# Merging float64 weights on VectorE with one instruction in place of three, with ScalarE and GpSimd preparing sign and low bits

## The chip, the cores and the metric

The kernel runs on one core of one Trainium2 chip. The metric is device time in microseconds (us); lower is better. One program does the whole computation. Its engines are PE (TensorE), DVE (VectorE), ACT (ScalarE), POOL (GpSimd) and SP (SyncE, which here issues every DMA). Each engine executes its own instructions strictly in the order in which the program holds them, and waits at an instruction until the semaphores it names have arrived, so whatever stands behind a waiting instruction on the same engine waits too.

## The reference

Attention with a threshold under the row maximum, for 8 batches of 8 heads with 576 positions of 64 values, and then a two-layer network with softplus in the middle on the 4608 resulting rows:

```python
scores = scale * np.matmul(q, k.transpose(0, 1, 3, 2))
thresh = np.max(scores, axis=-1, keepdims=True) - tau
scores = np.where(scores >= thresh, scores, -1000000000.0)
attn = np.exp(scores - max) / (sum + 1e-09)
attn_out = np.matmul(attn, v).astype(np.float32)
x = attn_out.transpose(0, 2, 1, 3).reshape(4608, 512)
h = x @ w_in                                  # w_in  512 x 2048, float64
g = np.maximum(h, 0.0) + np.log1p(np.exp(-np.abs(h)))
out = (g @ w_out).astype(np.float32)          # w_out 2048 x 512, float64
```

The two weight matrices come as float64, because they were divided by the square root of a numpy number. q, k and v are float32. The engines have no float64, so the kernel has to make float32 values out of the two 32-bit words of each weight.

## The kernel before, in words

**Attention.** The work is cut into 32 units of one batch and two heads. A unit has 9 tiles of 128 query rows, so there are 288 tiles, numbered through. A tile goes through these steps: scores on PE into one of two PSUM buffers called s (`scores`, L410); the negated row maximum `negm` on DVE (`row_max`, L416) and the threshold `thr`; the exponential into `e_all` on ACT (`exps`, L424); the mask and the row sum on DVE (`mask`, L429, which writes `e_all` again); the transpose of the masked weights on PE (`weights_T`, L460 and L463); copies of the transposed weights into a rounded part gH on ACT and a remainder gL (`weights_hi`, `weights_lo`); and the products with v on PE (`values`, L536 to L538). In the first 36 tiles (`TG = 36`) `thr` and the copies of gL are ACT's (L418, L483) and the remainder itself is made on PE (L511, L513: tile `tl`). From tile 36 on, gL and `thr` are DVE's (L125, L420), ACT copies gH alone (L485), and the transposes go back into the s buffer, which is free for the scores of a later tile only when gH and gL have been read out of it.

**The network.** From tile 41 on the matrix products of the two layers (L629 to L633 with `w_in`, L687 to L691 with `w_out`) are laid between the attention steps, a quota of them for every tile. Softplus is on ACT (L651) and needs another activation table than the exponential, hence the table loads around it.

**The weights.** The matrices are prepared in 32 blocks of 128x512 values, 16 of `w_in` (tiles `wc_i`, `wa_i`) and 16 of `w_out` (`wc_o`, `wa_o` or `ws_o`, `wo_o`). A new block is begun at every second tile, tiles 0 to 62, by the step "w" of a written order of steps per tile. `to_f32` loads the raw words of the block into `wc` by one DMA (L177) and then works in steps that are put off by a number of points (`defer`; there are two points in each of the first 36 tiles). Each weight has a high word (sign, exponent, upper bits of the fraction) and a low word. Before the change a block took:

- ACT, L185: the absolute value of the high word, read as a float32 and scaled, into `wa`;
- POOL, L186: a clamp of `wa` between two limits;
- DVE, L192: shift `wa` left by 3, which puts exponent and fraction in their float32 places;
- DVE, L194: take the sign bit out of the high word and put it in by a bitwise or;
- DVE, L197: shift the low word right by 29, so that three bits remain, and put them in by a bitwise or;
- POOL, L118 and L125: split the float32 value into the rounded part and the remainder that PE multiplies with. For `w_in` both are stored to a buffer in memory (SP, L226), from which the network loads them later (L613).

**What sets the order.** The code writes the steps of a tile in a fixed sequence, but a scheduler then lays out the instructions of each engine by its own estimates of when each could run. A changed instruction therefore moves its neighbours too, on all engines. The merging instructions on DVE are tied behind the last mask that was written (`behind(i, masked)`), which keeps them from being laid ahead of it.

## Time and profile before

| what | value |
|---|---|
| median of 3 runs | 1471.95 us (1471.4 to 1474.29) |
| the profiled execution's own time | 1474.09 us |
| its span, from the first to the last instruction | 1472.3 us |
| mean granted TensorE clock | 0.991 |
| busy share of the span: PE, DVE, ACT, POOL | 95%, 69%, 59%, 41% |
| HBM read and written | 140.51 MB, 27.41 MB |

In the groups of the profile a row reads: line, engine, operation, output tile, inputs, shapes, count, then busy time in us and the mean of one in ns, then the idle time of the engine just before and what ended it. Rows of windows give for each stretch of the span its length, the busy time of each engine with the number of instructions, the granted clock of PE (1.00 is full), the share of time in which the DMA engines were busy, and GB/s. Rows of waits read: engine, line, what it waited for, us in total, number of times, the longest. Rows of the timeline begin with the start and the duration in us. PE's matmuls are pipelined, so that the durations of neighbours overlap.

### The profile page before, as it was taken

The page shows a single profiled execution, that of the slowest core. Times are in us where ns is not written, and L with a number is a line of the kernel's source. Part 1 is how long each engine was busy: PE and PEld are TensorE (multiplying, and loading weights), DVE is VectorE, ACT ScalarE, POOL GpSimd, SP SyncE. Part 2 cuts the span into 40 slices and gives each one's busy share as a digit, 9 for nine tenths or more (in the row PEclk, how much of TensorE's full clock was granted, in tenths as well). Part 3 has the DMA queues.
Part 4 walks back from the last instruction along what each step waited for, and adds up shares of the span by engine and source line. Part 5 has one row for each costly group of instructions (what it writes and reads, how often), then busy time and mean ns, then how long its engine had stood idle before and what let it go on. Part 6 is the DMA issues. An engine that isn't in the chain of part 4 may idle for free.

```text
span 1472.3 us, 23929 instructions
## 1 busy us (share of the span) xinstructions
PE 1405.8 (95%) x8024; PEld 1192.3 (81%) x8024; DVE 1013.3 (69%) x2251; ACT 872.2 (59%) x1671; POOL 604.7 (41%) x629
## 2 busy tenths in 40 slices
PE   6878789999999999999999999999999999999998
PEld 5767677788888888888888888888888888788886
DVE  6998778877777777777777777777777777411211
ACT  6887577566766576656666666657665665411110
POOL 3767565544333433343334433343334332323221
PEclk9999899999999999999999999999999999999999
DMA  5777565434344554335334534454433533344321
GB/s 149 213 203 199 168 200 161 134 111 135 109 121 117 129 150 121 110 107 153 108 101 116 140 106 117 117 139 142 119 113 107 159 93 82 101 136 128 116 86 43
DMA packets 131210, 189.95 MB, mean 129 GB/s; under 512 B 35312, under 2 KB 86800, under 8 KB 131088
## 3 DMA queue, kind: packets, MB, share of 16 engines
q1 hardware_dynamic: 131088, 188.43, 44.2%
q8 instruction: 64, 1.05, 0.3%
q14 instruction: 58, 0.48, 0.1%
HBM read 140.51 MB, written 27.41 MB: 114 GB/s over the span
## 4 chain that ended last, share of the span: by engine, by line
PE 74%; DVE 8%; ACT 7%; issue 4%; POOL 3%; DMA 3%; SPq 1%; POOLq 0%; DVEq 0%; ACTq 0%
PE s L410 10%; PE h L631 8%; PE h L629 8%; PE h L633 8%; PE o L691 7%; PE o L689 7%; PE o L687 7%; PE s L463 7%; PE pv L536 3%; PE pv L537 3%; DVE negm L416 2%; PE tr L351 2%; DVE e_all L429 2%; POOL g L125 1%; DMA wc_i<-in_moe_w_in_dram 1%
## 5 line engine op out<-in xcount | busy, mean ns | idle before, releaser
L485 ACT CAST gH<-s 128x512 fp32r<-128x512 f32 (+1 forms) x448 | 186.7, 466 | 160.8 <-PE s L463 152.8
L125 POOL TENSOR_TENSOR g<-st,g 128x512 fp32r<-128x512 f32 x144 | 192.8, 1357 | 194.2 <-DVE g L122 182.3
L429 DVE SCALAR_TENSOR_TENSOR e_all<-s,thr,e_all 128x576 f32<-128x576 f32 x288 | 234.3, 815 | 37.8 <-ACT e_all L424 34.8
L416 DVE TENSOR_REDUCE negm<-s 128x1 f32<-128x576 f32 x288 | 217.4, 755 | 41.4 <-PE s L410 33.4
L691 PE MATMUL o<-wo_o,g 128*128 128x512 f32 x576 | 232.6, 404 | 5.3 <-POOL g L125 5.3
L631 PE MATMUL h<-xl,wi 128*128 128x512 f32 x576 | 233.1, 405 | 1.7 <-POOL xl L125 1.7
L687 PE MATMUL o<-wo_o,g 128*128 128x512 f32 x576 | 232.9, 404 | 1.0 <-ACT st L651 0.7
L629 PE MATMUL h<-xh,wi 128*128 128x512 f32 x576 | 230.6, 401 | 1.9 <-ACT st L651 1.4
L633 PE MATMUL h<-xh,wi 128*128 128x512 f32 x576 | 230.4, 400 | 0.0
L689 PE MATMUL o<-wo_o,g 128*128 128x512 f32 x576 | 229.7, 399 | 0.0
L424 ACT ACTIVATE e_all<-s,negm 128x576 f32<-128x576 f32 x288 | 215.8, 750 | 10.3 <-DVE negm L416 6.5
L125 DVE TENSOR_TENSOR gL<-s,gH 128x512 fp32r<-128x512 f32 (+1 forms) x280 | 175.0, 633 | 59.1 <-ACT gH L485 55.8
L410 PE MATMUL s<-kT,qT 128*128 128x288 f32 x1024 | 194.3, 311 | 13.3 <-DVE gH L125 5.9
L410 PEld LDWEIGHTS s<-kT,qT 128*128 128x128 f32 x1024 | 150.5, 192 | 33.9 <-issue 11.4
L122 DVE CAST g<-st 128x512 fp32r<-128x512 f32 x128 | 57.4, 485 | 149.6 <-ACT st L651 149.1
L463 PE MATMUL s<-identr,e_all 128*128 128x128 f32 x1008 | 155.7, 277 | 3.8 <-DVE e_all L429 3.8
L651 ACT ACTIVATE st<-h 128x512 f32<-128x512 f32 x144 | 78.3, 596 | 117.3 <-PE h L633 116.7
L536 PE MATMUL pv<-gH,vt 128*128 128x320 f32 (+1 forms) x512 | 143.9, 301 | 1.4 <-ACT gH L485 1.3
L537 PE MATMUL pv<-gL,vt 128*128 128x320 f32 (+1 forms) x512 | 142.8, 300 | 1.5 <-DVE gL L125 1.4
L691 PEld LDWEIGHTS o<-wo_o,g 128*128 128x128 f32 x576 | 108.7, 189 | 29.6 <-POOL g L125 11.0
L463 PEld LDWEIGHTS s<-identr,e_all 128*128 128x128 f32 x1008 | 116.2, 142 | 19.2 <-DVE e_all L429 10.9
L629 PEld LDWEIGHTS h<-xh,wi 128*128 128x128 f32 x576 | 108.9, 189 | 25.4 <-ACT st L651 1.9
(105 smaller groups left out, 2381.1 us busy)
## 6 DMA issues: line engine op xcount, KB each, us to landing
wi<-wi_d SPq DMA_DIRECT2D x144, 512.0 KB
qT<-qT SPq DMA_DIRECT2D x124, 128.0 KB
R<-r_d SPq DMA_DIRECT2D x64, 144.0 KB
kn<-in_k_dram SPq DMA_DIRECT2D x32, 256.0 KB
qn<-in_q_dram SPq DMA_DIRECT2D x32, 256.0 KB
vn<-in_v_dram SPq DMA_DIRECT2D x32, 256.0 KB
wc_i<-in_moe_w_in_dram SPq DMA_DIRECT2D x16, 512.0 KB
wi_d<-wc_i SPq DMA_DIRECT2D x32, 256.0 KB
```

The costliest lines, as they stand in the source:

```text
L125: eng.tensor_tensor(out=out_, in0=in_, in1=hi.bitcast(F32), op=ALU.subtract)
L410: nc.tensor.matmul(sp[:, hf, 0:HS], lhs, s.kT[j][:, k0 + hf * HS:k0 + (hf + 1) * HS], start=(m == 0), stop=(m == len(parts) - 1))
L416: nc.vector.reduce_max(negm, s.sp[t][:, :, 0:HS], axis=AX.XY, negate=True)
L424: nc.scalar.activation(e_all[:, s.half[t], :].rearrange("p (h n) -> p h n", h=2), s.sp[t][:, :, 0:HS], AF.Exp, bias=s.m[t][0], scale=1.0)
L429: masked.append(nc.vector.scalar_tensor_tensor(out=e2, in0=s.sp[t][:, :, 0:HS], scalar=s.m.pop(t)[1], in1=e2, op0=ALU.is_ge, op1=ALU.mult, ...
L463: nc.tensor.matmul(main[:, c, :], e[:, c0:c0 + P], ident, is_transpose=True, start=True, stop=True)
L629: nc.tensor.matmul(h, wi[:, 0, cc, :], u.h[cc], start=(cc == 0), stop=False)
L631: nc.tensor.matmul(h, wi[:, 0, cc, :], u.l[cc], start=False, stop=False)
L633: nc.tensor.matmul(h, wi[:, 1, cc, :], u.h[cc], start=False, stop=(cc == NCC - 1))
L687: nc.tensor.matmul(o, gh[:, sl], wo[fc][:, 0, :], start=(i == 0), stop=False)
L689: nc.tensor.matmul(o, gh[:, sl], wo[fc][:, 1, :], start=False, stop=False)
L691: nc.tensor.matmul(o, gl[:, sl], wo[fc][:, 0, :], start=False, stop=(i == QF - 1))
```

## The change

The low word of each weight is turned in place into a word that holds the sign in bit 31 and the three bits in bits 0 to 2. It is done by halves of 16 bits: ACT computes the low half from the high half (a scaled and rounded value, which is the three top bits), and POOL then writes the high half from a comparison of the high word with zero (32768 or 0). DVE shifts `wa` by 3 and merges the prepared word in the same instruction. The sequence per block is now: ACT L191 (low half), one point later ACT L195 (absolute value, as L185 before), POOL L196 (high half) and POOL L198 (clamp, as L186 before), `step` points later DVE L203 (the one merge), one point later the split on POOL. Before, the three DVE instructions were one point, `step` points and `step` points apart; `step` is 2 for the first blocks and 1 once half of the `w_out` pieces are held.

```diff
+    third = cpool.tile([P, 1], F32, name="third")
+    nc.vector.memset(third, 2.0 ** -14 - 0.5)
...
+        halves = words.bitcast(U16).rearrange("p (n t) -> p n t", t=4)
         words = words.rearrange("p (n t) -> p n t", t=2)
-        low, high = words[:, :, 0], words[:, :, 1]
+        low, high = words[:, :, 0], words[:, :, 1].bitcast(F32)
         mu = m.bitcast(U32)
         def first():
-            nc.scalar.activation(m, high.bitcast(F32), AF.Abs, scale=2.0 ** 16)
+            nc.scalar.activation(halves[:, :, 0], halves[:, :, 1], AF.Identity, scale=2.0 ** -13, bias=third)
+            later_(1, magnitude)
+
+        def magnitude():
+            nc.scalar.activation(m, high, AF.Abs, scale=2.0 ** 16)
+            nc.gpsimd.tensor_scalar(out=halves[:, :, 1], in0=high, scalar1=0.0, scalar2=32768.0,
+                                    op0=ALU.is_lt, op1=ALU.mult)
             nc.gpsimd.tensor_scalar(out=m, in0=m, scalar1=W_MAX, scalar2=W_MIN, op0=ALU.min, op1=ALU.max)
-            later_(1, lambda: second(0))
-        def second(n):
-            if n == 0:
-                i = nc.vector.tensor_scalar(out=mu, in0=mu, scalar1=3, scalar2=None, op0=ALU.logical_shift_left)
-            elif n == 1:
-                i = nc.vector.scalar_tensor_tensor(out=mu, in0=high, scalar=0x80000000, in1=mu,
-                                                   op0=ALU.bitwise_and, op1=ALU.bitwise_or)
-            else:
-                i = nc.vector.scalar_tensor_tensor(out=mu, in0=low, scalar=29, in1=mu,
-                                                   op0=ALU.logical_shift_right, op1=ALU.bitwise_or)
+            later_(step, second)
+
+        def second():
+            i = nc.vector.scalar_tensor_tensor(out=mu, in0=mu, scalar=3, in1=low,
+                                               op0=ALU.logical_shift_left, op1=ALU.bitwise_or)
             if took > 1:
                 behind(i, masked)
-            if n < 2:
-                later_(step, lambda: second(n + 1))
-            else:
-                later_(1, lambda: then(parts, w, done))
+            later_(1, lambda: then(parts, w, done))
```

Behind the changed lines all line numbers are larger by 3 in the changed kernel (the mask is L432 there, the exponential L427, gH L486, the split L122 and L129).

DVE's order around tile 4 of unit 4 (tile 40 of all), where gL and gH on DVE empty an s buffer that PE's next scores wait for. Before:

```order
L550 TENSOR_TENSOR xp_4_2042<-pv_4_0_2043,xp_4_2042 64x256
L429 SCALAR_TENSOR_TENSOR e_all_136,sums_4_1865<-s_1_138,thr_4_3_2034,e_all_136 128x576
L197 SCALAR_TENSOR_TENSOR wa_o5_1946<-wc_o5_1945,wa_o5_1946 128x512
L192 TENSOR_SCALAR wa_o6_2016<-wa_o6_2016 128x512
L416 TENSOR_REDUCE negm_4_4_2073<-s_0_137 128x1
L125 TENSOR_TENSOR gL_4_1_2031<-s_1_138,gH_4_1_2030 128x4x128
L420 TENSOR_SCALAR thr_4_4_2074<-negm_4_4_2073,ntau_85 128x1
L125 TENSOR_TENSOR gH_4_1_2030<-s_1_138,gH_4_1_2030 64x128 x2
L429 SCALAR_TENSOR_TENSOR e_all_136,sums_4_1865<-s_0_137,thr_4_4_2074,e_all_136 128x576
L194 SCALAR_TENSOR_TENSOR wa_o6_2016<-wc_o6_2015,wa_o6_2016 128x512
```

And the same place in the changed kernel:

```order
L432 SCALAR_TENSOR_TENSOR e_all_138,sums_4_1870<-s_1_140,thr_4_3_2037,e_all_138 128x576
L553 TENSOR_TENSOR xp_4_2046<-pv_4_0_2047,xp_4_2046 64x256
L419 TENSOR_REDUCE negm_4_4_2078<-s_0_139 128x1
L423 TENSOR_SCALAR thr_4_4_2079<-negm_4_4_2078,ntau_85 128x1
L129 TENSOR_TENSOR gL_4_1_2034<-s_1_140,gH_4_1_2033 128x4x128
L129 TENSOR_TENSOR gH_4_1_2033<-s_1_140,gH_4_1_2033 64x128 x2
L432 SCALAR_TENSOR_TENSOR e_all_138,sums_4_1870<-s_0_139,thr_4_4_2079,e_all_138 128x576
L203 SCALAR_TENSOR_TENSOR wa_o6_2019<-wa_o6_2019,wc_o6_2018 128x512
```

Two weight instructions stood between the mask of tile 3 and the reads of s_1 for tile 4, and a third behind the next mask; now there is none between them and one behind the next mask.

ACT's order where it handles the block `wc_i1_2`, in unit 1 (tiles 9 to 17 of all). In this early form of a tile ACT copies gH, PE makes `tl` from it and ACT copies gL from `tl`. Before, in tiles 1 to 3 of the unit:

```order
L483 ACTIVATE gL_1_0_652<-tl_1_1_698 128x4x128
L566 COPY rt_0_718<-rT_0_709 9x128
L185 ACTIVATE wa_i1_2_870<-wc_i1_2_869 128x512
L483 ACTIVATE gH_1_1_743<-tm_1_2_729 128x4x128
L418 ACTIVATE thr_1_3_725<-negm_1_3_724,ntau_85 128x1
L424 ACTIVATE e_all_136<-s_0_137,negm_1_3_724 128x576
L483 ACTIVATE gL_1_1_744<-tl_1_2_746 128x4x128
```

And in the changed kernel, in tiles 5 to 7 of the unit:

```order
L427 ACTIVATE e_all_138<-s_1_140,negm_1_6_886 128x576
L486 ACTIVATE gH_1_2_843<-tm_1_5_891 128x4x128
L191 ACTIVATE wc_i1_2_872<-wc_i1_2_872,third_102 128x512
L486 ACTIVATE gL_1_2_844<-tl_1_5_902 128x4x128
L195 ACTIVATE wa_i1_2_873<-wc_i1_2_872 128x512
L486 ACTIVATE xp_1_758<-pv_1_1_912 64x320
L421 ACTIVATE thr_1_7_934<-negm_1_7_933,ntau_85 128x1
L427 ACTIVATE e_all_138<-s_0_139,negm_1_7_933 128x576
```

The block's one activation stood in tile 2 of the unit; its two stand some three tiles later now, the first between gH and gL of tile 5 and the second right behind that gL. From tile 72 on the instructions stand in the same order on every engine and on SP's queue in both kernels.

More of the change, by code (lines that the diff above doesn't have):

```diff
@@ L12 @@
 U32 = mybir.dt.uint32
+U16 = mybir.dt.uint16
 AF = mybir.ActivationFunctionType
```

## The prediction

> **What bounds the kernel now.** I read the page first, for the engines and for the part of the span in which something is lost.
>
> ```profile
> span 1472.3 us, 23929 instructions
> PE 1405.8 (95%) x8024; PEld 1192.3 (81%) x8024; DVE 1013.3 (69%) x2251; ACT 872.2 (59%) x1671; POOL 604.7 (41%) x629
> ...
> PEclk9999899999999999999999999999999999999999
> ```
>
> PE is the bound of the whole, and an average says nothing on a change whose instructions all lie in tiles 0 to 63. So I cut the span where DVE's row maxima of tiles 4, 36, 42 and 68 begin and asked for windows: the first holds 32 tiles with blocks and no network, the second 6 tiles, the third 26 tiles with blocks and the network, the fourth is the same work without blocks.
>
> ```profile
> core 0: us, PE busy (x) PEld busy (x) DVE busy (x) ACT busy (x) POOL busy (x), PEclk, DMA share, GB/s
> 21.49:134.24 112.75, 92.50 (x654) 81.55 (x652) 102.28 (x199) 94.03 (x223) 72.38 (x83) 0.97 0.67 191
> 134.24:159.57 25.33, 19.26 (x127) 15.92 (x126) 23.78 (x53) 17.94 (x38) 19.35 (x21) 0.96 0.69 191
> 159.57:293.71 134.14, 121.16 (x655) 99.19 (x653) 108.10 (x226) 88.76 (x163) 79.11 (x84) 0.93 0.54 167
> 293.71:394.15 100.44, 98.48 (x583) 83.47 (x584) 76.39 (x178) 69.33 (x131) 41.24 (x44) 1.00 0.45 128
> ```
>
> In stretch one DVE is busy 91%, ACT 83%, PE 82%: DVE leads, but ACT is close behind. In stretch two DVE is at 94%. In stretch three PE is at 90% with a granted clock of 0.93, against 98% and 1.00 in stretch four. Scaling stretch four's PE time by the matmuls, stretch three's would take 98.48 x 655 / 583 = 110.6 us at the full clock. It took 134.14, so 23.5 us are lost there: 13.0 in which PE is idle, and 121.16 - 110.6 = 10.6 in which it runs at a lowered clock. With stretch four's idle share (1.96 us, or 2.2 scaled) left in, 21.3 us are the most that any change could win back in stretch three. What follows tile 68 is PE's and the same in both kernels.
>
> Next the waits of PE, first stretch one, then two and three together.
>
> ```profile
> PE tm L463 <- DVE e_all L429: 6.8, 4, 2.9
> PE tr L460 <- DVE e_all L429: 6.3, 5, 2.5
> PE tl L513 <- ACT gH L483: 5.3, 11, 1.4
> ...
> PE s L410 <- DVE gL L125: 5.7, 4, 3.8
> PE s L410 <- DVE gH L125: 5.5, 2, 3.5
> PE h L631 <- POOL xl L125: 1.7, 1, 1.7
> ```
>
> PE waits for DVE: 13.1 us for masks in stretch one, 11.2 us for the reads that empty an s buffer in two and three. The clock windows show what such a wait costs afterwards.
>
> ```profile
> 157.50:164.30 6.80, 5.61 (x19) 4.79 (x20) 5.71 (x15) 2.07 (x7) 2.07 (x4) 0.50 0.82 215
> 218.90:222.30 3.40, 3.40 (x12) 2.67 (x12) 2.48 (x6) 0.89 (x3) 3.32 (x5) 0.50 0.48 153
> 259.90:263.30 3.40, 3.40 (x14) 3.00 (x13) 2.70 (x7) 2.24 (x4) 3.32 (x4) 0.50 0.53 167
> ```
>
> ```profile
> 154.46 1.62 DVE L192 TENSOR_SCALAR wa_o<-wa_o 128x512 uint32<-128x512 uint32 x1
> ...
> 158.23 1.30 PE L410 MATMUL s<-kT,qT 128*128 128x288 f32 x4 [3.53 <-DVE gH L125]
> ...
> 164.02 0.42 DVE L192 TENSOR_SCALAR wa_o<-wa_o 128x512 uint32<-128x512 uint32 x1
> ...
> 218.85 1.29 PE L410 MATMUL s<-kT,qT 128*128 128x288 f32 x4 [3.77 <-DVE gL L125]
> ...
> 258.14 0.79 PE L410 MATMUL s<-kT,qT 128*128 128x288 f32 x4 [2.01 <-DVE gH L125]
> ```
>
> The half clock sets in around a wait of 2 to 4 us and lasts 3.4 or 6.8 us. At 154.46 the shift L192, which takes 0.42 us at 164.02, takes 1.62 us ahead of the reads for which PE then waits 3.53 us.
>
> **What the change removes and adds.** DVE's weight instructions, from the groups with their forms apart:
>
> ```profile
> L194 DVE SCALAR_TENSOR_TENSOR wa_i<-wc_i,wa_i 128x512 uint32<-128x512 uint32 x16 | 14.3, 892 | 0.1
> L192 DVE TENSOR_SCALAR wa_i<-wa_i 128x512 uint32<-128x512 uint32 x16 | 13.4, 837 | 0.1
> L197 DVE SCALAR_TENSOR_TENSOR wa_i<-wc_i,wa_i 128x512 uint32<-128x512 uint32 x16 | 12.2, 760 | 0.2
> L194 DVE SCALAR_TENSOR_TENSOR wa_o<-wc_o,wa_o 128x512 uint32<-128x512 uint32 x13 | 12.1, 930 | 0.1
> L197 DVE SCALAR_TENSOR_TENSOR wa_o<-wc_o,wa_o 128x512 uint32<-128x512 uint32 x13 | 11.1, 855 | 0.1
> L192 DVE TENSOR_SCALAR wa_o<-wa_o 128x512 uint32<-128x512 uint32 x13 | 8.9, 685 | 2.7 <-POOL wa_o L186 2.7
> ```
>
> These 87 take 72.0 us, 0.83 us each; the other nine (`ws_o`) are of the same forms. The new merge L203 has the shapes of L197, so 0.76 to 0.86 us as its rows stand; I take 0.83. A block then costs DVE 0.83 in place of 2.48 us: 1.65 less, 53 us over 32 blocks. By stretch (one block for two tiles): 16, 3 and 13 blocks, 26.4, 5.0 and 21.4 us. DVE in stretch one falls from 102.3 to 75.9, in three from 108.1 to 86.7.
>
> Added, with the nearest rows (the fifth, from L186's own answer, gives shortest, median and longest in ns):
>
> ```profile
> L185 ACT ACTIVATE wa_i<-wc_i 128x512 f32<-128x512 f32 x16 | 10.8, 672 | 7.6 <-DMA wc_i<-in_moe_w_in_dram 7.5
> L186 POOL TENSOR_SCALAR wa_i<-wa_i 128x512 f32<-128x512 f32 x16 | 12.0, 749 | 15.6 <-ACT wa_i L185 15.0
> L364 ACT ACTIVATE qT<-tr,qscale 128x512 fp32r<-128x512 f32 x64 | 44.5, 696 | 33.9 <-PE s L410 33.9
> L125 POOL TENSOR_TENSOR g<-st,g 128x512 fp32r<-128x512 f32 x144 | 192.8, 1357 | 194.2 <-DVE g L122 182.3
> L186 POOL TENSOR_SCALAR wa_o<-wa_o x13: 614/615/943, 67.0 to 263.4; 128x512 f32<-128x512 f32 x13
> L103 DVE TENSOR_SCALAR ntau<-tau_sb 128x1 f32<-128x1 f32 x1 | 0.2, 154 | 2.2 <-DMA tau_sb<-in_tau_dram 2.2
> ```
>
> No row shows 16-bit halves. L191 reads and writes 512 elements at a step of 8 bytes; L185 reads at that step (0.67), L364 has an operand per partition as L191 does (0.70). I take 0.68, with 0.67 and 0.75 as ends: 10.9, 2.0 and 8.8 us on ACT by stretch. POOL's L196 is of L186's kind, 0.75 (ends 0.62, what a clamp takes undisturbed, and 1.36, what POOL's two-input instructions take): 12, 2 and 10 us. POOL then stands at 84 of 112.75 in stretch one and 89 of 134 in three. It has room, and nobody but the merge and the split waits for L196, so I cost it at nothing; if POOL became late, PE's 1.7 us wait for `xl` would be the one to grow. The one memset, of 128x1, lies at the start, where DVE waits 2.2 us for tau (L103). The block's chain is shorter by `step` points and longer by one activation. On SP's queue the raw words of blocks 3 and 4 are now issued behind the first stores of split weights, which wait for POOL. The activation that waits for them has slipped by about three tiles too (the order above), so I cost that at nothing as well; its cover gone, ACT would wait as in L185's row, 7.5 us in all already.
>
> **Stretch one.** ACT becomes the fullest engine: 94.0 + 10.9 = 104.9 us of 112.75. Its 18.7 us of idle time are in good part these:
>
> ```profile
> ACT gL L483 <- PE tl L513: 6.0, 12, 2.1
> ACT gH L483 <- PE tm L463: 3.5, 2, 1.9
> ACT thr L418 <- DVE negm L416: 3.0, 4, 1.5
> ACT wa_i L185 <- DMA wc_i<-in_moe_w_in_dram: 2.3, 3, 1.1
> ```
>
> The waits for `tm` and `negm`, 6.5 us, are DVE's lateness passed on and should go. The 6.0 for `tl` is the round trip from gH over PE, and the new order puts activations of weights into it (L191 between gH and gL); I take 4 of it as filled. So 104.9 + 18.7 - 6.5 - 4 = 113.1: nothing is won, 0.4 lost, which I call 0. Bounds: ACT without a gap, 104.9, wins 7.9; ACT with all its gaps kept, 123.6, loses 10.9.
>
> **Stretch two.** DVE at 94% loses 5.0 us of work, and the 3.53 us wait at 158.23, with two weight instructions ahead of the reads, has none there in the new order: 3.5 us won (0 to 5).
>
> **Stretch three.** Two thirds of the blocks' DVE time go. If the loss followed it, 2/3 x 21.3 = 14.2 us come back; but ACT goes from 88.8 to 97.6 and POOL to 89 in a shorter stretch, so I take 12.5, between the half (10.6) and two thirds. Bounds: 0 and 21.3.
>
> **Sum.** 0 - 3.5 - 12.5 = -16 us against the profiled execution's 1474.1: 1458.1. The median of the runs shown, 1471.95, is 2.1 lower, which makes 1456.0.
>
> The Trainium skill speaks partly against this: "SBUF — State Buffer", section "Who interferes with whom", says that a DVE instruction with two SBUF inputs and a GpSimd instruction that reads SBUF shut each other out for the whole instruction. The merge has two such inputs and there are 32 more POOL instructions. By that rule I estimate 1.2 us a merge, so 12 us more DVE time, 5 of it in stretch three, and a sum nearer 1459. The 1.62 us shift above agrees with such a lock; but 64 instructions that can be locked out go away, and the rows of L197 already hold this cost.
>
> **The rivals.** *All of DVE's lateness goes.* Stretch one then runs at ACT's 104.9 (-7.9), two gives 4 and three 21.3: -33 us, 1439. For it: every long wait of PE after 150 us is named DVE. Against: POOL and ACT are fuller than in stretch four, and a stretch without any gap is seen nowhere before tile 68. Chance 0.2.
>
> *DVE was only where the lateness showed.* PE's, ACT's and DVE's work hang in one chain, so that the waits move to ACT's gH and the time stays: 1472, within 3 us. For it: ACT waits for `tl` and PE for gH (5.3) even now. Against: the fourth stretch, with ACT at 69% and DVE at 76%, leaves PE idle for 1.96 us alone. Chance 0.1.
>
> *ACT's queue takes DVE's place, and it is slower.* In stretch one each L191 pushes back the exponential or gH behind it, none of the gaps is filled: +10.9. In stretch three an activation of 0.68 before gH holds the s buffer as the shift did: 13 x 0.68 = 8.8 off the gain, which leaves 3.7, and 3.5 of stretch two. 10.9 - 3.7 - 3.5 = +3.7, and 29 x 0.22 = 6.4 more if L191 takes 0.9 us in 16-bit form; 1476 to 1482. It decides from the point at which ACT in stretch one is longer than about 128 us. For it: ACT is a strict queue and would be at 93%. Against: the 6.5 us handed on by DVE. Chance 0.12.
>
> **How the numbers follow.** My forecast, a gain of 8 to 24 us, has 0.58; its own range is 1448 to 1464. The range 1438 to 1472 takes in the first rival at its full size and reaches to no change, and leaves out some 0.15. A change under 0.2% (2.9 us) can't be told from none here. Faster is 0.58 + 0.2 = 0.78, same 0.1, slower 0.12.
>
> **What would show it.** Right: DVE's weight rows 32 of about 0.83 us; DVE in stretch one near 76 us and ACT near 105 of about the same length; the granted clock of the third stretch above 0.96, its length near 120; PE's waits for gL and gH on DVE under 5 us; the same 1178 us behind tile 68. Wrong: PE `tl` waiting for ACT's gH over 10 us, an activation L191 over 0.9 us, merges over 1.2 us, or long waits of ACT for the raw words.

## The result and the profile after

The changed kernel takes 1507.87 us (median of four runs, 1507.55 to 1508.74) against 1471.68 us for the kernel before on the same chip (1471.06 to 1474.29): ratio 1.0243, 95% interval 1.0226 to 1.0261. It is 36 us slower, or 2.4%. The forecast was 1456.0 with a range of 1438 to 1472, and faster with a chance of 0.78; sign and range were both missed.

The page of the changed kernel, its span, its row for the engines and the granted clock by slices:

```profile
span 1506.4 us, 23982 instructions
...
PE 1414.5 (94%) x8024; PEld 1200.6 (80%) x8024; DVE 970.4 (64%) x2188; ACT 909.9 (60%) x1703; POOL 678.1 (45%) x661
...
PEclk9979889999999999999999999999999999999999
```

DVE does get 43 us less to do (1013.3 before) and 63 instructions fewer. But the clock drops in slices 3, 5 and 6, and POOL has gained 73 us and ACT 38, where the prediction put in 24 and 22.

For the comparison by stretches the cuts must lie where DVE's row maxima of the same tiles begin in both kernels. The prediction's cuts lay one tile early: the starts of tiles 4, 36, 42 and 68 before are 26.47, 137.43, 165.18 and 294.62 us. The windows of the kernel before at these cuts, and then those of the changed kernel (length, busy time by engine with counts, granted clock, DMA share, GB/s):

```profile
26.47:137.43 110.96, 91.93 (x652) 81.08 (x651) 101.43 (x198) 92.42 (x220) 73.03 (x84) 0.97 0.68 189
137.43:165.18 27.75, 21.43 (x123) 17.68 (x122) 24.54 (x54) 16.80 (x37) 19.18 (x21) 0.88 0.70 193
165.18:294.62 129.44, 116.81 (x641) 95.70 (x640) 105.02 (x217) 86.82 (x158) 77.76 (x82) 0.95 0.53 165
```

```profile
27.01:167.53 140.52, 101.14 (x651) 88.03 (x650) 78.17 (x171) 111.74 (x237) 106.92 (x100) 0.90 0.58 164
167.53:197.17 29.64, 23.38 (x125) 20.34 (x123) 21.11 (x44) 20.43 (x39) 26.61 (x24) 0.80 0.46 135
197.17:330.16 132.99, 115.90 (x649) 95.31 (x649) 90.00 (x196) 102.64 (x172) 107.33 (x95) 0.97 0.55 165
```

Nearly all of the loss is in the first stretch: 110.96 became 140.52. From tile 68 to the end the changed kernel takes 1506.4 - 330.16 = 1176.2 us, the kernel before 1472.3 - 294.62 = 1177.7. In the first stretch no engine is full any more: PE 72%, DVE 56%, ACT 80%, POOL 76%. Time is lost in waits between engines, and their rows in the groups say which:

```profile
L203 DVE SCALAR_TENSOR_TENSOR wa_i<-wa_i,wc_i 128x512 uint32<-128x512 uint32 x16 | 13.3, 834 | 21.1 <-POOL wa_i L198 21.1
L203 DVE SCALAR_TENSOR_TENSOR wa_o<-wa_o,wc_o 128x512 uint32<-128x512 uint32 x13 | 12.5, 960 | 9.9 <-POOL wa_o L198 9.8
L203 DVE SCALAR_TENSOR_TENSOR ws_o<-ws_o,wc_o 128x512 uint32<-128x512 uint32 x3 | 2.1, 692 | 7.5 <-POOL ws_o L198 7.5
...
L191 ACT ACTIVATE wc_i<-wc_i,third 128x512 uint16<-128x512 uint16 x16 | 23.3, 1457 | 7.2 <-DMA wc_i<-in_moe_w_in_dram 7.2
L191 ACT ACTIVATE wc_o<-wc_o,third 128x512 uint16<-128x512 uint16 x16 | 23.3, 1457 | 3.8 <-DMA wc_o<-in_moe_w_out_dram 3.8
...
L196 POOL TENSOR_SCALAR wc_o<-wc_o 128x512 uint16<-128x512 f32 x16 | 43.6, 2724 | 11.1 <-ACT wc_o L191 11.1
L196 POOL TENSOR_SCALAR wc_i<-wc_i 128x512 uint16<-128x512 f32 x16 | 43.0, 2686 | 15.2 <-ACT wc_i L191 15.0
```

Read the two numbers behind the bar first: total and mean. L191 takes 1.457 us, not 0.68; L196 takes 2.70 us, not 0.75. The merge is what the prediction said, (13.3 + 12.5 + 2.1) / 32 = 0.87 us. Then the idle time at the end of the rows: DVE, the engine that was to be relieved, stands idle 38.5 us ahead of the 32 merges. Of these, 38.4 us, at 21 of the merges, end with POOL's clamp L198, which stands behind L196 on POOL's queue.

One block of the changed kernel shows the whole chain, in the timeline (start, duration, engine, line; idle time before in brackets):

```profile
112.75 1.47 ACT L191 ACTIVATE wc_o<-wc_o,third 128x512 uint16<-128x512 uint16 x1
...
114.30 2.69 POOL L196 TENSOR_SCALAR wc_o<-wc_o 128x512 uint16<-128x512 f32 x1 [2.65 <-ACT wc_o L191]
...
116.43 0.77 ACT L427 ACTIVATE e_all<-s,negm 128x576 f32<-128x576 f32 x1
...
116.82 0.41 POOL L122 TENSOR_SCALAR q<-qn 128x256 fp32r<-128x256 f32 x1
...
117.31 0.72 POOL L129 TENSOR_TENSOR q<-qn,q 128x256 fp32r<-128x256 f32 x1
...
118.11 0.61 POOL L198 TENSOR_SCALAR wa_o<-wa_o 128x512 f32<-128x512 f32 x1
...
118.76 0.69 DVE L203 SCALAR_TENSOR_TENSOR wa_o<-wa_o,wc_o 128x512 uint32<-128x512 uint32 x1 [3.29 <-POOL wa_o L198]
...
119.37 0.81 DVE L432 SCALAR_TENSOR_TENSOR e_all<-s,thr,e_all 128x576 f32<-128x576 f32 x1
...
120.34 0.30 PE L463 MATMUL tr<-identr,e_all 128*128 128x128 f32 x1 [2.10 <-DVE e_all L432]
...
120.67 0.74 ACT L427 ACTIVATE e_all<-s,negm 128x576 f32<-128x576 f32 x1 [1.73 <-PE tr L463]
```

POOL waits for L191 and then works 2.69 us on the sign half. The scheduler has laid a split of q behind it, 1.2 us more. So the clamp starts at 118.11 only, and the merge, at the head of DVE's queue for 3.29 us, at 118.76. The mask stands behind the merge and starts at 119.37, though the exponential that it masks had ended at 117.2; PE waits 2.10 us for it, and behind PE ACT waits 1.73. Right after, PE's clock is halved, as it is in ten windows of 3.4 or 6.8 us before the last matmuls of this kernel (six in the kernel before):

```profile
121.53:124.95 3.42, 3.42 (x20) 3.24 (x18) 2.08 (x5) 3.42 (x7) 2.46 (x3) 0.50 0.34 128
```

In the waits of the changed kernel up to 168 us (total, number of times, longest) the same chain is at the top:

```profile
DVE wa_i L203 <- POOL wa_i L198: 20.8, 9, 4.0
...
PE tm L466 <- DVE e_all L432: 16.0, 10, 4.7
...
PE tr L463 <- DVE e_all L432: 11.0, 5, 3.8
```

PE's waits for masks are 27.0 us here, against 13.1 in the prediction's rows of before.

### The profile page after: what moved, and what is told of

Read it like the earlier page. It is cut to its first block, busy times and chain, and to the rows that moved or that the text cites. A ratio compares the mean times of both kernels' runs of the same rounds, so it can differ in the third digit from the quotient of the medians.

```text
span 1506.4 us, 23982 instructions
## 1 busy us (share of the span) xinstructions
PE 1414.5 (94%) x8024; PEld 1200.6 (80%) x8024; DVE 970.4 (64%) x2188; ACT 909.9 (60%) x1703; POOL 678.1 (45%) x661
## 4 chain that ended last, share of the span: by engine, by line
PE 72%; ACT 7%; POOL 6%; DVE 5%; issue 4%; DMA 4%; SPq 2%; POOLq 0%; ACTq 0%; DVEq 0%
PE s L413 9%; PE h L634 8%; PE h L632 8%; PE h L636 8%; PE o L694 7%; PE o L692 7%; PE o L690 7%; PE s L466 7%; PE pv L539 3%; PE pv L540 3%; PE tr L354 2%; POOL g L129 1%; ACT L654 1%; POOL wc_i L196 1%; ACT e_all L427 1%
## 5 line engine op out<-in xcount | busy, mean ns | idle before, releaser
L129 POOL TENSOR_TENSOR g<-st,g 128x512 fp32r<-128x512 f32 x144 | 192.1, 1351 | 194.3 <-DVE g L126 184.4
L432 DVE SCALAR_TENSOR_TENSOR e_all<-s,thr,e_all 128x576 f32<-128x576 f32 x288 | 234.2, 816 | 42.9 <-ACT e_all L427 39.6
L427 ACT ACTIVATE e_all<-s,negm 128x576 f32<-128x576 f32 x288 | 215.8, 749 | 11.1 <-PE tr L463 5.3
L129 DVE TENSOR_TENSOR gL<-s,gH 128x512 fp32r<-128x512 f32 (+1 forms) x280 | 175.0, 633 | 58.1 <-ACT gH L488 54.5
```

Source lines behind the costliest of these rows:

```text
L129: eng.tensor_tensor(out=out_, in0=in_, in1=hi.bitcast(F32), op=ALU.subtract)
L427: nc.scalar.activation(e_all[:, s.half[t], :].rearrange("p (h n) -> p h n", h=2), s.sp[t][:, :, 0:HS], AF.Exp, bias=s.m[t][0], scale=1.0)
L432: masked.append(nc.vector.scalar_tensor_tensor(out=e2, in0=s.sp[t][:, :, 0:HS], scalar=s.m.pop(t)[1], in1=e2, op0=ALU.is_ge, op1=ALU.mult, ...
```

## The experiments

Two things are new in the path, and each could carry the loss: ACT's longer queue (46.6 us of L191), or POOL's L196 with the waits behind it. A third theory is that the merge or the new order of the steps costs by itself. All edits are to the changed kernel, unless said otherwise. Times are medians; ratios are to the kernel before on the same chip, with 95% intervals. The kernel before was at 1473.3 to 1474.7 us on the three chips used, so small differences are better read from the ratios.

An edit can also move its neighbours, because the scheduler lays out the engines anew. So the order matters below: by it is meant the sequence of operations and tiles on each engine in the trace, up to tile 72 and without the added instruction. Where two kernels have the same order, the difference in time belongs to the edited instruction alone.

### The price of each form

Added to the end of the kernel before, rows of instructions of one form each; `o` and `i` are output and input.

```diff
+        for _ in range(3):
+            nc.scalar.activation(o, i, AF.Identity, scale=2.0 ** -13, bias=bias)
...
+        for _ in range(3):
+            eng.tensor_scalar(out=o, in0=i, scalar1=0.0, scalar2=32768.0,
+                              op0=ALU.is_lt if cmp else ALU.min, op1=ALU.mult if cmp else ALU.max)
```

> The kernel before, with a row of instructions behind its end, three of each form, on 128x512 elements (ACT: L191's shape, then the same with a 32-bit output, with a packed 16-bit output, with packed 32-bit input, and all 32-bit; POOL: L196's shape, then 32-bit and packed outputs, and min/max in place of the comparison; VectorE: L196's shape and a 32-bit output). Theory A (it is the 16-bit operands at a step of 8 bytes): ACT 1.4 to 1.5 us in L191's shape and under 0.8 with 32-bit operands at the same step; POOL 2.7 us in L196's shape and under 0.8 with a 32-bit output. Theory B (POOL's time is that of the comparison, whatever the output): POOL 2.7 us for the comparison with a packed 32-bit output too, and about 0.7 for min and max. Theory C (both are long only because the engines were crowded in that place): every form under 0.9 us here, where nothing else runs.

The groups of that kernel (`mraw` is at a step of 8 bytes, `mflat` packed):

```profile
L972 POOL TENSOR_SCALAR mraw<-mraw 128x512 uint16<-128x512 f32 x3 | 8.1, 2695 | 0.2
L972 POOL TENSOR_SCALAR mraw<-mflat 128x512 uint16<-128x512 f32 x3 | 7.9, 2626 | 0.2
...
L972 POOL TENSOR_SCALAR mraw<-mraw 128x512 f32<-128x512 f32 x3 | 6.0, 1989 | 0.2
L972 POOL TENSOR_SCALAR mflat<-mraw 128x512 uint16<-128x512 f32 x3 | 5.9, 1953 | 0.2
...
L968 ACT ACTIVATE mraw<-mflat,third 128x512 uint16<-128x512 f32 x3 | 4.4, 1465 | 0.0
L968 ACT ACTIVATE mraw<-mraw,third 128x512 uint16<-128x512 uint16 x3 | 4.3, 1442 | 0.2
L968 ACT ACTIVATE mraw<-mraw,third 128x512 f32<-128x512 f32 x3 | 2.3, 758 | 0.0
L968 ACT ACTIVATE mflat<-mraw,third 128x512 uint16<-128x512 uint16 x3 | 2.3, 755 | 0.1
...
L972 DVE TENSOR_SCALAR mraw<-mraw 128x512 uint16<-128x512 f32 x3 | 2.2, 729 | 33.4 <-POOL mraw L972 33.4
...
L972 DVE TENSOR_SCALAR mflat<-mraw 128x512 f32<-128x512 f32 x3 | 1.4, 456 | 0.0
```

and its rows of min and max alone, from a window that holds only those three:

```profile
L972 POOL TENSOR_SCALAR mflat<-mraw 128x512 f32<-128x512 f32 x3 | 1.9, 646 | 0.2
```

On ACT theory A holds: only the form that writes 16 bits at a step of 8 bytes is long (1.44 to 1.47 us). The read doesn't matter, nor does a packed 16-bit output (0.755). On POOL it is A and B together: 0.646 us for min and max becomes 1.92 to 1.99 with the comparison, for packed and for 32-bit output, and 2.63 to 2.70 when the output is 16 bits at that step. Theory C is out, though not as it was planned: the scheduler laid these rows at 1268 to 1342 us, beside matmuls and other work of the network, so the place was not empty. But the long forms are as long here as in the changed kernel, and the short ones next to them are short. So my row for L196, a clamp, was of the right shape and of the wrong operation, and of the wrong output.

### One added instruction at a time

With both left out:

```diff
-            nc.scalar.activation(halves[:, :, 0], halves[:, :, 1], AF.Identity, ...)
-            nc.gpsimd.tensor_scalar(out=halves[:, :, 1], in0=high, ..., op0=ALU.is_lt, op1=ALU.mult)
-                                               op0=ALU.logical_shift_left, op1=ALU.bitwise_or)
+                                               op0=ALU.logical_shift_left, op1=ALU.bitwise_and)
```

> The changed kernel without both half-word instructions (L191 and L196 left out, so signs and low bits of the weights are not made; the merge ands the raw low word in place of or-ing it). What is left of the change: two of DVE's three instructions gone, the block's steps in the new order. Theory POOL (the long L196 on POOL's queue delays the clamp, for which DVE's merge then waits): 1448 to 1462, a gain of 10 to 24 us, and DVE's wait for the clamp under 8 us. Theory ACT (the 46.6 us of L191 on the fullest engine): the same 1448 to 1462. Rival ORDER (the merge, or the new order of the block's steps, costs by itself): 1480 to 1510.

1455.66 us, ratio 0.9875 (0.9851 to 0.9899); DVE waits 4.2 us for the clamp. The merge and the new order together win 18.8 us, and theory ORDER falls.

With L196 alone left out (of the edit above all but its first line):

> The changed kernel without L196 on POOL (so the signs are not made; the merge ands in place of or-ing); L191 on ACT stays with its 1.457 us. Theory POOL: most of the loss goes, 1455 to 1475. Theory ACT: most of the loss stays, 1490 to 1507, with PE waiting for gH and tl.

1475.59 us, ratio 1.0006 (0.9992 to 1.0020), just above what theory POOL expected and far from theory ACT.

With L191 alone left out (of the edit above the first line alone):

> The changed kernel without L191 on ACT (so the low bits are not rounded; the raw low half is or-ed in); L196 on POOL stays with its 2.70 us. Theory POOL: most of the loss stays, 1488 to 1505, and DVE still waits 25 us or more for the clamp. Theory ACT: most of the loss goes, 1455 to 1475.

1494.43 us, ratio 1.0135 (1.0116 to 1.0154), as theory POOL expected. DVE waits 30.3 us for the clamp. The first stretch of the three (both left out; ACT's kept; POOL's kept), from the windows:

```profile
26.31:131.46 105.15, 92.88 (x656) 81.60 (x655) 75.17 (x167) 91.55 (x221) 69.61 (x85) 0.97 0.70 199
```

```profile
27.91:149.97 122.06, 99.45 (x649) 85.39 (x648) 76.13 (x166) 109.00 (x235) 70.34 (x86) 0.93 0.64 181
```

```profile
27.44:152.62 125.18, 98.05 (x656) 86.16 (x655) 77.17 (x166) 93.24 (x221) 107.13 (x99) 0.92 0.59 166
```

DVE has 75 to 77 us of work in all three. ACT's instruction adds 17 us to this stretch and 19.9 to the whole; POOL's adds 20 to the stretch and 38.8 to the whole; together they add 52.2 (1507.87 less 1455.66, from two comparisons between which the kernel before differed by 3 us), a little less than the sum. So POOL's carries about two thirds of the loss and ACT's one third: without ACT's part the kernel would still be slower than before, and without POOL's it would be no better than before.

The 38.8 us are POOL's instruction and nothing else: with and without it, PE, DVE and ACT execute the same order, and POOL and SP all but the same. The 19.9 us of ACT's instruction hold a new order too: with it, some 140 of DVE's 465 instructions and 100 of ACT's 454 stand in other places. What ACT's length does by itself is shown below, at the low prices.

### A control for the data

Since the and leaves most weights near zero, the merge alone was run with full mantissas (the weights are still not the right ones: sign and shift by 3 are left out).

```diff
-            i = nc.vector.scalar_tensor_tensor(out=mu, in0=mu, scalar=3, in1=low,
-                                               op0=ALU.logical_shift_left, op1=ALU.bitwise_or)
+            i = nc.vector.scalar_tensor_tensor(out=mu, in0=low, scalar=29, in1=mu,
+                                               op0=ALU.logical_shift_right, op1=ALU.bitwise_or)
```

> As the kernel with the merge alone, but the merge shifts the low word right by 29 and ors it to the magnitude, as L197 did before, so that the weights are ordinary numbers with full mantissas (signs and the shift by 3 left out). A control for the data: the and in the earlier experiment made most weights nearly zero. If the 1455.7 us came from the work left out and not from the numbers multiplied: 1452 to 1460. If it came from nearly empty operands: over 1466.

1456.82 us, ratio 0.9888 (0.9872 to 0.9904). The order is the same on all engines, and the numbers multiplied make no difference that can be told from the noise.

### POOL: the wait, or the load

To the control, POOL's long instruction added behind the clamp, where the merge needn't wait for it:

```diff
             nc.gpsimd.tensor_scalar(out=m, in0=m, scalar1=W_MAX, scalar2=W_MIN, op0=ALU.min, op1=ALU.max)
+            nc.gpsimd.tensor_scalar(out=halves[:, :, 3], in0=high, scalar1=0.0, scalar2=32768.0,
+                                    op0=ALU.is_lt, op1=ALU.mult)
```

> The control with the merge alone (the merge shifts the low word right and ors it; signs and the shift by 3 left out), and POOL's long instruction added behind the clamp, not ahead of it, writing into halves that the merge doesn't read. POOL does the same work as in the changed kernel (2.7 us for each block). Theory WAIT (what costs is that the merge at the head of DVE's queue waits for the clamp behind the long instruction): near the control, 1456 to 1468, with DVE's waits for the clamp under 15 us. Theory LOAD (POOL is full in the first 36 tiles, and everything behind its long instructions is late: clamps of the next block, splits, and with the splits the stores and the loads behind them): 1480 to 1495, as with the sign half alone (1494.4).

1471.51 us, ratio 0.9988 (0.9978 to 0.9998), between the two expectations. DVE's merge still waits 16.4 us in all for the clamp. At its longest wait, 3.6 us, the clamp stands on POOL behind the long instruction and the split of the block before and behind the split of k:

```profile
L202 DVE SCALAR_TENSOR_TENSOR wa_i<-wc_i,wa_i 128x512 uint32<-128x512 uint32 x16 | 14.3, 893 | 6.8 <-POOL wa_i L195 6.7
...
L202 DVE SCALAR_TENSOR_TENSOR wa_o<-wc_o,wa_o 128x512 uint32<-128x512 uint32 x13 | 10.0, 772 | 6.4 <-POOL wa_o L195 6.3
...
L202 DVE SCALAR_TENSOR_TENSOR ws_o<-wc_o,ws_o 128x512 uint32<-128x512 uint32 x3 | 2.1, 693 | 3.4 <-POOL ws_o L195 3.4
```

The same instruction on POOL costs 14.7 us behind the clamp (against the control) and 38.8 ahead of it (against the merge alone). The place, and not the load, is the larger part, about 24 us; the 14.7 hold some of that wait, and also a moved order (69 of DVE's 465 instructions).

The changed kernel, nothing left out, with the merge later:

```diff
-            later_(step, second)
+            later_(step + 4, second)
```

> The changed kernel with the merge four points later in the program, nothing left out. Theory WAIT: the clamp has ended by then, DVE's idle time ahead of L203 falls from 38.5 us to under 12, and the time falls to 1475 to 1490 (the activation's 20 us stay). Theory LOAD: POOL is no less full and the split only moves back, 1498 to 1512.

1501.82 us, ratio 1.0199 (1.0186 to 1.0212): by the total LOAD would be right. The stretches say otherwise. First and third window of this kernel:

```profile
26.81:152.92 126.11, 100.85 (x656) 86.23 (x654) 80.20 (x167) 110.64 (x237) 109.10 (x98) 0.92 0.61 173
...
182.91:322.05 139.14, 117.14 (x644) 94.92 (x643) 89.57 (x195) 103.03 (x171) 107.80 (x96) 0.96 0.51 156
```

In the first stretch 14.4 of the 29.6 us lost come back (140.52 to 126.11), which is near the 122.06 that ACT's instruction leaves by itself: WAIT is right there. The third stretch loses 6.2 more (132.99 to 139.14). Its waits:

```profile
DVE gL L129 <- ACT gH L488: 24.7, 16, 4.6
...
DVE ws_o L203 <- POOL ws_o L198: 14.0, 4, 5.8
```

The blocks in `ws_o` are those that `to_f32` doesn't put off at all (`later_` runs their steps at once when `took` is 1 or less). The edit can't reach them, there are four of them in place of three, and each holds DVE's queue for 3.5 us on average (2.5 in the changed kernel). ACT also waits longer for raw words, 22.7 us ahead of L191 against 11.0; that the pieces held longer are the reason is likely, but was not tried by itself.

### At the prices that the prediction took

```diff
-            nc.scalar.activation(halves[:, :, 0], halves[:, :, 1], AF.Identity, scale=2.0 ** -13, bias=third)
+            nc.scalar.activation(low, low, AF.Identity, scale=2.0 ** -29, bias=third)
...
-            nc.gpsimd.tensor_scalar(out=halves[:, :, 1], in0=high, ..., op0=ALU.is_lt, op1=ALU.mult)
+            nc.gpsimd.tensor_scalar(out=high, in0=high, scalar1=0.0, scalar2=1.0, op0=ALU.mult, op1=ALU.mult)
```

> The changed kernel with both added instructions kept in their places, but at about the prices the prediction took: the low bits written as a whole 32-bit word by ACT (0.75 us by the measured form, in place of 1.46), the sign word on POOL as high times 0.0 in 32 bits (0.65 to 0.75 us by the version before, in place of 2.70), and one merge. The sign word isn't merged, so signs are left out. Theory PRICE (the prediction's working holds and only the two prices were wrong): 1453 to 1462. Theory DOSE (each added us on ACT and POOL costs in proportion, so that costing POOL's at nothing was wrong whatever the price): 1455.7 + 24 / 46.6 x 20 + 0.68 / 2.70 x 38.8 = 1476, so 1468 to 1480.

1466.52 us, ratio 0.9951 (0.9933 to 0.9969), between the two expectations. Three of its rows:

```profile
L202 DVE SCALAR_TENSOR_TENSOR wa_i<-wa_i,wc_i 128x512 uint32<-128x512 uint32 x16 | 13.4, 837 | 9.3 <-POOL wa_i L197 9.2
...
L191 ACT ACTIVATE wc_i<-wc_i,third 128x512 uint32<-128x512 uint32 x16 | 12.5, 782 | 7.4 <-DMA wc_i<-in_moe_w_in_dram 7.4
...
L196 POOL TENSOR_SCALAR wc_i<-wc_i 128x512 f32<-128x512 f32 x16 | 10.7, 668 | 15.2 <-ACT wa_i L195 15.0
```

ACT's instruction takes 0.78 us here and POOL's 0.66. And without POOL's, the line of `high` left out of that edit:

> The same with POOL's sign word left out as well: ACT's 0.75 us and the single merge alone. PRICE: 1454 to 1460. DOSE: 1455.7 + 10 = 1466, so 1463 to 1470.

1464.96 us, ratio 0.9941 (0.9927 to 0.9956), as DOSE expected. In this pair of kernels the two theories divide by engine. On ACT it is DOSE: 0.78 us a block costs 9.3 us and 1.457 costs 19.9, both about 0.4 of the time added. The second step is ACT's length alone: this kernel and the one with ACT's half at its full price execute the same order on all engines, and they differ by 10.6 us (1475.59 - 1464.96), or 0.0065 in the ratio, for 22 us more on ACT. On POOL it is PRICE here: 0.66 us costs 1.6 us, which is within the uncertainty of the two (32 of DVE's 465 instructions moved as well), and 2.70 costs 32.3 (1507.87 - 1475.59, beside L191, in nearly the same order). A later pair of versions says otherwise for POOL (below). The windows of the kernel at both low prices:

```profile
26.96:141.66 114.70, 91.50 (x647) 79.74 (x646) 77.71 (x167) 101.40 (x235) 80.67 (x101) 0.98 0.65 189
141.66:169.11 27.45, 22.23 (x128) 18.57 (x128) 20.03 (x48) 18.70 (x41) 19.35 (x24) 0.89 0.70 199
169.11:287.74 118.63, 110.67 (x647) 92.08 (x646) 90.56 (x196) 95.94 (x173) 81.39 (x94) 1.00 0.62 185
```

This is nearly the kernel that the prediction worked out (0.78 us on ACT for its 0.68, 0.66 on POOL for its 0.75): 3.7 us lost in stretch one (forecast 0), 0.3 won in two (3.5), 10.8 won in three (12.5).

### How much of DVE's relief counts

In the kernel before, the sign instruction alone left out:

```diff
-            elif n == 1:
-                i = nc.vector.scalar_tensor_tensor(out=mu, in0=high, scalar=0x80000000, in1=mu, ...)
```

> The kernel before with the middle one of DVE's three instructions (L194, the sign) left out and nothing added: 26.5 us less on DVE, so signs are left out. If the relief is in proportion, half of the 18 us that two instructions won: 1463 to 1467. If only the first of the two counts (DVE is no longer the last to end): 1456 to 1461. If the second counts (DVE stays the last until it falls below ACT): 1469 to 1474.

1457.49 us, ratio 0.9895 (0.9877 to 0.9912). One instruction less wins 16 us, nearly the 18.8 of the merge alone with two less. Its first and third stretch:

```profile
26.73:134.11 107.38, 90.25 (x652) 79.51 (x651) 88.34 (x182) 92.66 (x221) 72.86 (x87) 0.98 0.72 197
...
158.68:277.05 118.37, 110.23 (x645) 91.34 (x646) 93.51 (x210) 88.50 (x162) 74.31 (x82) 1.00 0.64 189
```

DVE is busy 88.34 us in a first stretch of 107.38, against 75.17 in 105.15 with the merge alone; the third stretch is 118.37 us against 122.61. That DVE was no longer what ended last beyond the first 26 us is a likely reason, but not a shown one: the two kernels also differ in the order of a block's steps, and against the kernel before some 200 of ACT's 454 instructions stand elsewhere in either.

### Versions with nothing left out

If one instruction less is enough, two instructions on DVE and one cheap added one elsewhere should win. ACT with whole words, DVE with two:

```diff
-            nc.scalar.activation(halves[:, :, 0], halves[:, :, 1], AF.Identity, scale=2.0 ** -13, bias=third)
+            nc.scalar.activation(low, low, AF.Identity, scale=2.0 ** -29, bias=third)
...
-            nc.gpsimd.tensor_scalar(out=halves[:, :, 1], in0=high, ..., op0=ALU.is_lt, op1=ALU.mult)
...
+            else:
+                i = nc.vector.scalar_tensor_tensor(out=mu, in0=high.bitcast(U32), scalar=0x80000000, in1=mu,
+                                                   op0=ALU.bitwise_and, op1=ALU.bitwise_or)
```

> A version with nothing left out: ACT rounds the low bits as whole 32-bit words (0.75 us), POOL has nothing added, DVE needs two instructions (the shift with the low bits, then the sign with its mask). By PRICE: the relief of one instruction less and nothing for ACT, 1462 to 1468. By DOSE: 9 us won on DVE and 10 us lost on ACT, 1472 to 1478.

1474.08 us, ratio 1.0003 (0.9994 to 1.0013), as DOSE expected. POOL with the sign word (`high` times 0.0), DVE with two:

```diff
-            nc.scalar.activation(halves[:, :, 0], ...)
-            nc.gpsimd.tensor_scalar(out=halves[:, :, 1], in0=high, ..., op0=ALU.is_lt, op1=ALU.mult)
+            nc.gpsimd.tensor_scalar(out=high, in0=high, scalar1=0.0, scalar2=1.0, op0=ALU.mult, op1=ALU.mult)
...
+            if n == 0:
+                i = nc.vector.scalar_tensor_tensor(out=mu, in0=mu, scalar=3, in1=high.bitcast(U32),
+                                                   op0=ALU.logical_shift_left, op1=ALU.bitwise_or)
+            else:
+                i = nc.vector.scalar_tensor_tensor(out=mu, in0=low, scalar=29, in1=mu,
+                                                   op0=ALU.logical_shift_right, op1=ALU.bitwise_or)
```

> A version with nothing left out: POOL makes the sign word as high times 0.0, in 32 bits and in place (one multiplication, which takes 0.42 to 0.75 us in the kernel before, in place of 2.70), ACT has nothing added, and DVE needs two instructions: the shift with the sign or-ed in, and the low bits with their own shift as before. From the measured ends: one instruction less on DVE for each block wins half of what two won (18.8 us), 9; 0.65 us on POOL costs 0.65 / 2.70 of the sign half's 38.8 us by theory LOAD, 9, and under 4 by theory WAIT, where what counts is the clamp's delay beyond the merge's place. So 1470 to 1476 by LOAD, 1465 to 1470 by WAIT. If the multiplication is as slow as the comparison with a 32-bit output (1.95 us): over 1480.

1473.41 us, ratio 1.0000 (0.9988 to 1.0013), as LOAD expected and not WAIT, though DVE waits only 8.6 us for the clamp. Neither wins. The same without the sign word:

```diff
-            nc.gpsimd.tensor_scalar(out=high, in0=high, scalar1=0.0, scalar2=1.0, op0=ALU.mult, op1=ALU.mult)
...
-                i = nc.vector.scalar_tensor_tensor(out=mu, in0=mu, scalar=3, in1=high.bitcast(U32),
-                                                   op0=ALU.logical_shift_left, op1=ALU.bitwise_or)
+                i = nc.vector.scalar_tensor_tensor(out=mu, in0=mu, scalar=3, in1=low,
+                                                   op0=ALU.logical_shift_left, op1=ALU.bitwise_and)
```

> The version with the sign word on POOL and two DVE instructions, without the sign word: POOL has nothing added, and both DVE instructions stay in form and place (the first ands the low word in, so signs are left out and most weights are nearly zero). Theory ADDED (the 0.7 us on POOL ate the gain): 1456 to 1461, like the kernel before without L194. Theory PLACE (the first DVE instruction, of two inputs, two to three points into the block, is what costs): 1468 to 1475.

1467.64 us, ratio 0.9951 (0.9936 to 0.9966). Both theories seem to have a part: from 0.9895 to 0.9951 with the place and form of the first DVE instruction, from there to 1.0000 with the 0.7 us on POOL. That is some 7 us for POOL's 0.7, where it was 1.6 for 0.66 above. Some 75 of DVE's 497 instructions stand elsewhere between the last two, so the instruction and the order are not separated. So, with the sign word, the steps were put back to the cadence of the kernel before:

```diff
         def first():
-            later_(1, magnitude)
+            magnitude()
...
-            later_(step, second)
+            later_(1, second)
```

> A version with nothing left out: the sign word on POOL in 32 bits and two DVE instructions, at the cadence of the kernel before (activation, sign word and clamp in the block's first step, the first DVE instruction one point later). Theory PLACE: 1459 to 1466. Theory ADDED: 1470 to 1476.

1467.17 us, ratio 0.9947 (0.9934 to 0.9960), a little above what PLACE expected: this version beats both kernels, by 7.5 us the one before and by 40 the changed one. Another order of the two merges:

```diff
-                i = nc.vector.scalar_tensor_tensor(out=mu, in0=mu, scalar=3, in1=high.bitcast(U32),
-                                                   op0=ALU.logical_shift_left, op1=ALU.bitwise_or)
+                i = nc.vector.scalar_tensor_tensor(out=low, in0=low, scalar=29, in1=high.bitcast(U32),
+                                                   op0=ALU.logical_shift_right, op1=ALU.bitwise_or)
...
-                i = nc.vector.scalar_tensor_tensor(out=mu, in0=low, scalar=29, in1=mu,
-                                                   op0=ALU.logical_shift_right, op1=ALU.bitwise_or)
+                i = nc.vector.scalar_tensor_tensor(out=mu, in0=mu, scalar=3, in1=low,
+                                                   op0=ALU.logical_shift_left, op1=ALU.bitwise_or)
```

> As the version before it, but the first DVE instruction joins the low bits with the sign word and so doesn't need the clamp, which is behind the sign word on POOL; the second shifts the magnitude and ors them in. By the wait for the clamp (3.6 us for wa_i in the first such version, 8.6 in all): 2 to 4 us faster than the version before it; 1457 to 1464 by PLACE, 1468 to 1474 by ADDED.

1466.82 us, ratio 0.9949 (0.9935 to 0.9963), the same; the 2 to 4 us expected of it did not come, and it lies between the two ranges. Of the 16 us that one instruction less won, these two versions keep half. What takes the other half isn't settled. One candidate is the first merge, next to POOL's work, here in the version with the old cadence:

```profile
L202 DVE SCALAR_TENSOR_TENSOR wa_i<-wa_i,wc_i 128x512 uint32<-128x512 uint32 x16 | 18.4, 1151 | 3.9 <-POOL wa_i L196 3.7
```

It takes 1.15 us, where the one-input shift in its place before took 0.84. Another is DVE's wait for the clamp, 15.0 us in this version against 6.6 in the kernel before without L194. But neither ranks the versions: the slower one before it, at 1473.41 us, had a shorter first merge (1.04) and the shorter wait (8.6).

## Why the prediction was wrong

**What held.** The single merge: 0.83 forecast, 0.87 measured. DVE in stretch one: 76 forecast, 78.2 measured. The tail: the same within 1.5 us. The relief as a whole: the kernel with the merge and no added work stands at 1455.7 and 1456.8, where the prediction's 1456.0 stood. That agreement is luck, since that sum had a cost for ACT in it: by stretches the kernel wins 5.8, 4.1 and 6.8 us, not 0, 3.5 and 12.5. The caution on the lock between DVE and POOL (the Trainium skill, "SBUF — State Buffer", section "Who interferes with whom") gave an estimate of 1.2 us a merge; the mean of 0.87 us in this kernel, with 73 us more of POOL work beside it, speaks against so much, and the sum went rightly by the rows of L197. Single merges did take up to 1.76 us. The shift of 1.62 us that the prediction set beside the rule has one such input, not two.

**The steps that failed** are the two prices, and POOL's cost taken as nothing. Of the 51.9 us between forecast and result, 41.4 lie between the kernel at the low prices (1466.52) and the changed one, and 10.5 in the rest of the working (from two chips, on which the kernel before differs by 1.6 us). *L191* was sized at 0.68 us from rows that only read at a step of 8 bytes; it writes at that step too, in 16 bits, and took 1.457, outside the ends of 0.67 and 0.75. By itself it costs 19.9 us, of which 10.6 are the longer time. The slower rival had ACT's part and the branch ("if L191 takes 0.9"), and its 1476 to 1482 begins where the kernel with ACT's half alone came out (1475.59), in part by luck, as it took at most 0.9 us; but this was left out of the range, and no rival had POOL's part. The Trainium skill, "ScalarE: Activation LUTs", section "What ACT_TABLE_LOAD costs", puts an activation at one element per cycle and lane, fp32 and bf16 alike, from which I estimate 0.71 us for 512 values with an operand per partition. Of the seven forms measured, five lie at 0.72 to 0.76, near it; the two that write 16 bits at a step of 8 bytes take twice that, and there the measurement decides.

*L196* was sized at 0.75 us from the clamp, with 1.36 as the upper end, and costed at nothing. It took 2.70. At 0.66 us, "nothing" is right within the noise in the kernel that the prediction worked out; at 2.70 it costs 32 to 39. "Nobody but the merge and the split waits for L196" was true and not enough: the clamp L198 stands behind it on POOL, the merge waits for the clamp at the head of DVE's queue, and the masks stand behind the merge. An engine with a quarter of its time free can still be late.

**Smaller misses.** At nearly the forecast's own prices the kernel takes 1466.5, not 1456: ACT's time in stretch one isn't filled into its gaps as taken there (13.3 us stay idle of 114.70, where 8.2 were taken, and about 0.4 of ACT's added time shows at the end), and 0.3 us are won in stretch two instead of 3.5. Of the four signs named as proof against, one showed, an L191 over 0.9 us. PE's wait for gH was 6.5 us in the first stretch, the merges stayed under 1.2 on average, and ACT's wait for raw words was 11.0 in all. The sign that would have mattered, DVE waiting for the clamp, was not on the list. Of the signs for it, the third stretch had its clock of 0.97 but not its length (132.99 us, not 120), and PE's waits for gL and gH on DVE were 9.4 us behind the first stretch, not under 5.

## What to carry to other kernels

Before work is moved to another engine, find a row of the same operation with the same output type and step, not just the same shape; where there is none, let the upper end cover a multiple, or measure the form first. An added instruction on a queue with room is not free when the head of a busy queue waits behind it, and what it costs does not follow its length: ahead of the clamp, 0.66 us cost 1.6 us over 32 blocks in one kernel and 0.7 us about 7 in another, whose order moved too, while 2.70 us cost over 30. And see how much of a relief counts before paying for all of it: leaving out one DVE instruction won 16 us, two with the new order of steps 18.8.

## What the hardware showed that was not expected

- Writing 16-bit values at a step of 8 bytes doubles ACT's activation of 128x512 (0.755 to 1.44 us) and adds 0.7 us on POOL (1.99 to 2.70). On DVE it takes 0.729 us where packed 32-bit output takes 0.456; type and step were not tried apart there. Packed 16-bit output, 16-bit input at that step and 32-bit output at that step add nothing on ACT.
- POOL's comparison with a multiplication takes 1.95 us where min and max take 0.646 (both to packed 32-bit output), and a multiplication by two constants 0.66 (L196 at the low prices), all on 128x512.
- PE's granted clock fell to half in the changed kernel's ten places without PE having stood idle all the time: in the 3.41 us before each of them it was busy between 0 and 1.87 us (1.31 us before the window at 121.53). In the kernel before it was between 0.08 and 1.73 us before each of the six.
